# Eight experts after local attention: experts 2 to 7 in the order of their token counts, with slot lists cut by place

## The chip, the core and the metric

The kernel runs on one core of one Trainium2 chip. A core has five engines with queues of their own: TensorE (PE, with its weight loads shown apart as PEld), VectorE (DVE), ScalarE (ACT), GpSimd (POOL) and SyncE (SP), which here issues nearly all plain transfers. The metric is the time of one execution on the device in microseconds, as a median of runs; lower is better. Beside it stands one execution taken by the hardware profiler, from which all rows come.

## The reference

Attention over 4 batches, 8 heads and 768 positions, where a query sees the 96 positions up to its own and 8 global ones, with a bias by distance. Its output, 3072 tokens of 512 numbers, goes through a mixture of 8 experts, of which each token takes the two with the highest noisy logits:

```python
logits = x @ w_gate
noisy_logits = logits + np.log1p(np.exp(x @ w_noise)) * noise
top2 = np.argpartition(-noisy_logits, 2, axis=1)[:, :2]
# top2_w: softmax over the two chosen logits
for e in range(E):
    for k in range(2):
        mask = top2[:, k] == e
        h = np.maximum(x[mask] @ w1[e], 0.0)
        out[mask] += top2_w[mask, k, None] * (h @ w2[e])
```

w1[e] is 512 x 1024 and w2[e] 1024 x 512, in fp32. The experts share 6144 places in all, 768 each on average, but how many tokens an expert has is known only once the logits are.

## The kernel before

**Attention and routing.** Tokens go in 24 tiles of 128. While attention runs, route() works off five segments of tiles: it finds the two best experts of each token, counts per expert with matmuls against a triangle of ones (the running counts are kept in `carry`), and so gives each token a slot in its expert's list. A table of marks and entries multiplied on PE turns this round into `tab`, the token number of each slot; find() fills empty slots with rows of zeros and writes the result as integers, `ids`, of shape 128 x 8 experts x 8 tiles.

**An expert.** Every expert has 812 slots: a first list of 512 (4 tiles, `CA`) and a second of 300 (2 tiles and one of 44 rows, `CB`). gather() fetches the tokens of a tile by `ids` through POOL's queue; ready() and rest() split them into a high and a low fp16 half on DVE and ACT; turn() transposes a tile with a DMA that SP issues into `xx[0]` or `xx[1]`. The weights come as four quarters of 1 MB (`raw`, five buffers, load_w() on SP's queue), are scaled by powers of two (scales()) and split in halves too (split(): `w1h`, `w1l`, `w2h`, `w2l`). Products of halves replace fp32: three fp16 matmuls for one.

On PE an expert is: up(e, 0, f) for f = 0 to 7 (12 matmuls of 512 columns each, L857), up(e, 1, f) (12 of 300 columns), down(e, t) for 4 tiles (24 matmuls each, L890), then down_t(e, d) for d = 0 to 3, in which the weights stand still and the 300 slots move (24 matmuls each, L900), and back(e, t), which transposes its result again (4 transposes a tile, L911) while the next expert's up(e, 0, ...) runs. Behind each up step ACT writes `hh` = relu in fp16 (L867) and DVE `hl`, the rest (L868), out of one PSUM bank: bank "at" (two buffers) for even f, "sc" (three) for odd. put() (L874, L875) scales the rows and adds them to the output by an indirect DMA on POOL.

**What sets the order.** It is written out by hand: the loops over f, t and d at the end of the program say behind which PE step each step() of the next expert's weights, each gather, ready, rest and turn stands. An engine works its instructions off in that order. Expert 0 begins on tokens of the first 16 tiles, before all is routed, and experts 0 to 7 follow one another. At the end, if an expert had more tokens than slots, a serial part (behind the branch at L1032) computes those left over, by the counts in `carry` and the weights in `over`.

Of the kernel before, what the change touches and what calls it, by code (L numbers as in the profile page):

```python
# [20 lines left out]
P = 128  # L21
# [5 lines left out]
CAP = CA + CB  # L27
DUMP = 512
# [7 lines left out]
def tile_local_global_attention_then_moe(  # L36
# [60 lines left out]
    ids = consts.tile([P, E, TT + 1], I32, name="ids")  # L97
    ids0 = consts.tile([P, 1, TA], I32, name="ids0")
# [27 lines left out]
    asked = []  # L126

    def load_w(n=1):
        for _ in range(n):
# [3 lines left out]
            asked.append(order[len(asked)])  # L133
            if x == 1:
                t = wts.tile([P, KC, F // 2], F32, name="raw", tag="raw", bufs=5)
                src = w1[e, :, h * F // 2:(h + 1) * F // 2].rearrange("(k p) f -> p k f", p=P)
            else:
                t = wts.tile([P, FC // 2, Dm], F32, name="raw", tag="raw", bufs=5)
                src = w2[e, h * F // 2:(h + 1) * F // 2].rearrange("(k p) d -> p k d", p=P)
# [74 lines left out]
    def height(t):  # L214
        return P if t < TT - 1 else ML

    def rows(e, t):
        return (ids if e or t >= TA else ids0)[:height(t), e, t:t + 1]

    def gather(e, t, n=DUMP + N):  # L220
        xg[e, t] = gp.tile([height(t), Dm + E], F32, name="xg", bufs=5)
# [11 lines left out]
    def ready(e, t):  # L233
        x = xg[e, t]
        m = height(t)
# [9 lines left out]
    def rest(e, t):  # L245
        x = xg.pop((e, t))
        m = height(t)
# [8 lines left out]
    def turn(e, t):  # L256
        nc.sync.dma_start_transpose(out=place(t, P if t < TT - 1 else MP), in_=xp.pop((e, t)))

    def turn_pe(e, t, ps=None):
        x = xp.pop((e, t))  # L260
        m = height(t)
# [42 lines left out]
    def route(r):  # L304
# [80 lines left out]
        nc.vector.scalar_tensor_tensor(over[:, a:z], po, float(CAP), wd, op0=OP.is_ge, op1=OP.mult)  # L385
# [42 lines left out]
        if r + 1 == len(SEG):  # L428
            find(ids, slice(0, E), slice(0, TT + 1))
# [12 lines left out]
    with ExitStack() as actx:  # L442
# [114 lines left out]
        def route_consts():  # L557
# [21 lines left out]
            for x in tab, l1, wv:  # L579
                nc.vector.memset(x, 0.0)  # L580

# [259 lines left out]
    with ExitStack() as mctx:  # L841
# [9 lines left out]
        def up(e, c, f, spared=False, between={}):  # L851
            ps = (bank("sc", 3) if f % 2 else bank("at", 2))[:, :hh[c].shape[2]]
            fs = slice(f * P, (f + 1) * P)
            n = 0
            for k in range(KC):
                for w, x in ((w1h, 0), (w1h, KC), (w1l, 0)):
                    nc.tensor.matmul(ps, w[e % 2][:, k, fs], xx[c][:, x + k, :hh[c].shape[2]], start=n == 0, stop=n == 3 * KC - 1)  # L857
# [3 lines left out]
            if spared:  # L861
                h = mw.tile([P, 512], F32, name="h")[:, :hh[c].shape[2]]
                nc.scalar.activation(h, ps, AF.Relu)
                nc.scalar.activation(hh[c][:, f], h, AF.Copy)
                nc.gpsimd.tensor_sub(hl[c][:, f], h, hh[c][:, f])
                return
            nc.scalar.activation(hh[c][:, f], ps, AF.Relu)  # L867
            nc.vector.scalar_tensor_tensor(hl[c][:, f], ps, 0.0, hh[c][:, f],  # L868
                                           op0=OP.max, op1=OP.subtract)

        def put(e, t, ps):
            m = height(t)
# [21 lines left out]
        def down_t(e, d):  # L894
            ps = bank("av", 2)[:, :CB]
            cols = slice(d * P, (d + 1) * P)
            n = 0
            for f in range(FC):
                for w, x in ((w2h, hh), (w2h, hl), (w2l, hh)):
                    nc.tensor.matmul(ps, w[e % 2][:, f, cols], x[1][:, f], start=n == 0, stop=n == 3 * FC - 1)  # L900
                    n += 1
            if d % 2:
                nc.vector.tensor_copy(yt[:, d], ps)
            else:
                nc.scalar.activation(yt[:, d], ps, AF.Copy)

        def back(e, t):
            m = height(TA + t)
# [57 lines left out]
        for f in range(FC):  # L966
# [20 lines left out]
        for e in range(1, E):  # L987
            last = e + 1 == E
            for f in range(FC):
                up(e, 0, f)  # L990
                if f < TB:
# [5 lines left out]
            weigh(e, 0, TT)  # L997
            for f in range(FC):
# [5 lines left out]
                if not last:  # L1004
                    if f in (4, 6):
                        ready(e + 1, f // 2 - 2)
                    if f in (5, 7):
                        rest(e + 1, f // 2 - 2)
                        turn(e + 1, f // 2 - 2)
                        gather(e + 1, f // 2 + 3)  # L1010
            steps = [(down, t) for t in range(TA)]
            steps_t = [(down_t, d) for d in range(KC)]
            for j, (f, t) in enumerate(steps_t + steps if last else steps + steps_t):
                f(e, t)
                if not last:
                    if j < TA + TB - 2:
                        ready(e + 1, j + 2)
                    step(e + 1, [1, 3, 3, 3, 1, 1, 1, 1][j])
                    if j < TA + TB - 2:
                        rest(e + 1, j + 2)  # L1020
                        turn(e + 1, j + 2)
                elif j in (KC, KC + 1, KC + 2):
# [5 lines left out]
    nc.vector.tensor_scalar(cf[:, :E], carry[:1], -float(CAP), 0.0, op0=OP.add, op1=OP.max)  # L1028
# [3 lines left out]
    with tc.If(left > 0), tc.tile_pool(name="lc", bufs=1) as lc:  # L1032
        nc.sync.dma_start(past.rearrange("(t p) e -> p t e", p=P), over)
        for e in range(E):
            n = nc.values_load(more[0:1, e:e + 1], min_val=0, max_val=N)
            with tc.If(n > 0):
# [4 lines left out]
                with tc.For_i(0, NT, 1) as i:  # L1041
# [20 lines left out]
                    for f in range(FC):  # L1062
                        nc.tensor.matmul(ps, ht[:, f], wb[:, f], start=f == 0, stop=f == FC - 1)
                    nc.scalar.activation(y, ps, AF.Copy, scale=r[:, e:e + 1])
# [42 lines left out]
```

## Time and profile before

| | |
|---|---|
| median of 3 runs | 744.93 us (744.08 to 745.27) |
| the profiled execution | 747.32 us, its span 745.6 us |
| PE busy, of the span | 715.7 us (96%), 6199 matmuls |
| DVE busy | 485.2 us (65%) |
| ACT busy | 346.4 us (46%) |
| POOL busy | 208.3 us (28%) |
| mean granted clock of PE | 0.982 |

The span runs from the first to the last instruction. Busy times of single matmuls overlap, since matmuls are pipelined: what a group of them costs is read from the chain of waits, whose pieces don't overlap, and not from the mean of one. A DVE row whose bracket says "idle before" shows how long the engine waited ahead of it and for whom.

### The profile page before, as it was taken

How to read it: one execution, taken by the hardware profiler on the slowest of the kernel's cores; microseconds unless marked ns; L12 is line 12 of the kernel's file. 1: busy time of each engine (PE TensorE's matmuls, PEld its weight loads, DVE VectorE, ACT ScalarE, POOL GpSimd, SP SyncE). 2: the span in 40 equal slices, each digit the busy share in tenths (PEclk: the TensorE clock that was granted, in tenths of full speed). 3: DMA queues.
4: the chain of work that ended last, by engine and by line, in shares of the span. 5: the costliest groups of instructions: out<-in, count | busy, mean ns of one | idle time of the engine just before them, and what ended most of it. 6: DMA issues, size and time to landing. Idle time of an engine off the chain costs nothing.

```text
span 745.6 us, 16302 instructions
## 1 busy us (share of the span) xinstructions
PE 715.7 (96%) x6199; PEld 448.6 (60%) x6199; DVE 485.2 (65%) x1655; ACT 346.4 (46%) x744; POOL 208.3 (28%) x201
## 2 busy tenths in 40 slices
PE   7999978996999999999999999999999999999995
PEld 5887757775446746465555646464655556464762
DVE  7658896888697828655873767286558737672500
ACT  5887776675435434524252433345242524333401
POOL 2000184230346650313223121503132231212014
PEclk9999998898999999999999999999999999999999
DMA  7889794765519783784597558539945973642015
GB/s 223 267 271 279 241 291 146 231 224 207 207 41 166 218 179 114 136 156 93 163 144 127 170 104 183 106 116 132 161 94 161 137 134 119 99 69 34 1 20 75
DMA packets 107671, 112.56 MB, mean 151 GB/s; under 512 B 53216, under 2 KB 66224, under 8 KB 107584
## 3 DMA queue, kind: packets, MB, share of 16 engines
q1 hardware_dynamic: 95104, 84.25, 41.8%
q0 software_dynamic: 11936, 26.92, 21.0%
q8 instruction: 51, 0.84, 0.5%
q14 instruction: 36, 0.29, 0.1%
q10 hardware_dynamic: 544, 0.26, 0.1%
HBM read 71.61 MB, written 28.10 MB: 134 GB/s over the span
## 4 chain that ended last, share of the span: by engine, by line
PE 70%; issue 12%; DVE 11%; POOL 2%; ACT 2%; DMA 1%; POOLq 0%; SPq 0%; ACTq 0%; DVEq 0%
PE av L890 17%; PE at L857 15%; PE sc L857 14%; PE av L900 10%; PE av L664 4%; PE at L637 3%; POOL out_dram L875 2%; PE sc L616 2%; DVE ns L623 2%; DVE entry L409 1%; PE sc L285 1%; DVE wmx L149 1%; PE sc L293 1%; PE lg L299 1%; DVE xr L672 1%
## 5 line engine op out<-in xcount | busy, mean ns | idle before, releaser
L875 POOL DMA_INDIRECT out_dram<-y,ids x56 | 88.2, 1575 | 213.0 <-ACT y L874 208.8
L857 PEld LDWEIGHTS <-w1h 128*128 128x128 f16 x1024 | 99.8, 98 | 68.5 <-issue 0.8
L857 PE MATMUL at<-xx,w1h 128*128 128x300 f16 (+1 forms) x512 | 127.9, 338 | 0.0
L857 PE MATMUL sc<-xx,w1h 128*128 128x300 f16 (+1 forms) x512 | 126.2, 335 | 0.0
L222 POOL DMA_INDIRECT xg<-xd,ids x56 | 57.5, 1027 | 162.0 <-DVE hl L868 124.2
L890 PE MATMUL av<-w2h,hh 128*128 128x512 f16 x256 | 97.1, 379 | 0.0
L890 PE MATMUL av<-w2l,hh 128*128 128x512 f16 x256 | 97.0, 379 | 0.0
L890 PE MATMUL av<-w2h,hl 128*128 128x512 f16 x256 | 97.0, 379 | 0.0
L626 ACT ACTIVATE a<-ns,mx 128x168 f32<-128x168 f32 (+1 forms) x192 | 69.6, 421 | 41.3 <-DVE mx L623 40.5
L857 PE MATMUL at<-xx,w1l 128*128 128x512 f16 (+1 forms) x256 | 86.3, 337 | 0.0
L857 PE MATMUL sc<-xx,w1l 128*128 128x512 f16 (+1 forms) x256 | 85.8, 335 | 0.0
L890 PEld LDWEIGHTS <-hh 128*128 128x128 f16 x512 | 49.5, 98 | 56.0
L868 DVE SCALAR_TENSOR_TENSOR hl<-sc,hh 128x300 f16<-128x300 f32 (+1 forms) x63 | 36.3, 577 | 67.5 <-ACT hh L867 67.4
L149 DVE TENSOR_REDUCE wmx<-raw 128x1 f32<-128x1024 f32 x64 | 76.6, 1207 | 0.0
L900 PE MATMUL av<-hh,w2h 128*128 128x300 f16 x256 | 74.6, 291 | 0.0
L900 PE MATMUL av<-hh,w2l 128*128 128x300 f16 x256 | 74.3, 290 | 0.0
L900 PE MATMUL av<-hl,w2h 128*128 128x300 f16 x256 | 74.1, 290 | 0.0
L857 PEld LDWEIGHTS <-w1l 128*128 128x128 f16 x512 | 50.3, 98 | 37.9 <-issue 0.5
L867 ACT ACTIVATE hh<-at 128x300 f16<-128x300 f32 (+1 forms) x62 | 31.1, 502 | 89.1 <-PE at L857 89.1
L868 DVE SCALAR_TENSOR_TENSOR hl<-at,hh 128x300 f16<-128x300 f32 (+1 forms) x62 | 35.5, 573 | 52.6 <-ACT hh L867 52.6
L242 ACT ACTIVATE xp<-xg,up 128x512 f16<-128x512 f32 x48 | 34.5, 719 | 70.8 <-DVE up L240 60.6
L900 PEld LDWEIGHTS <-w2h 128*128 128x128 f16 x512 | 50.0, 98 | 16.5
(173 smaller groups left out, 1242.2 us busy)
## 6 DMA issues: line engine op xcount, KB each, us to landing
raw<-in_w SPq DMA_DIRECT2D x32, 1024.0 KB, 7.5
out_dram<-zero SPq DMA_DIRECT2D x14, 512.0 KB, 6.1
vs<-in_v SPq DMA_DIRECT2D x24, 260.0 KB, 3.4
xd<-xr SPq DMA_DIRECT2D x24, 256.0 KB, 7.9
qs<-in_q SPq DMA_DIRECT2D x23, 256.0 KB, 5.3
ks<-in_k SPq DMA_DIRECT2D x19, 272.0 KB, 9.5
vp<-in_v SPq DMA_DIRECT2D x20, 195.0 KB, 3.8
ks<-in_k SPq DMA_DIRECT2D x4, 464.0 KB, 4.6
```

The lines of the kernel that those rows point to most:

```text
L149: nc.vector.tensor_reduce(m[:, i:i + 1], t[:, i % 2 * n:(i % 2 + 1) * n], op=OP.max, axis=AX.X, apply_absolute_value=True)
L222: nc.gpsimd.indirect_dma_start(out=xg[e, t], out_offset=None, in_=xd[:n], in_offset=bass.IndirectOffsetOnAxis(ap=rows(e, t), axis=0), boun ...
L242: nc.scalar.activation(y[:m, :Dm], x[:, :Dm], AF.Copy, scale=u)
L626: nc.scalar.activation(A[m][:, s * w:(s + 1) * w], ns[:, s, :w], AF.Exp, bias=mx[:, s:s + 1], scale=-1.0)
L637: nc.tensor.transpose(ps[:, j * P:(j + 1) * P], x[:, a:a + P], ident)
L664: nc.tensor.matmul(ps[y * Q:(y + 1) * Q, h % 4], w, t, start=id(x) in first, stop=id(x) in final, tile_position=(r, y * Q))
L857: nc.tensor.matmul(ps, w[e % 2][:, k, fs], xx[c][:, x + k, :hh[c].shape[2]], start=n == 0, stop=n == 3 * KC - 1)
L867: nc.scalar.activation(hh[c][:, f], ps, AF.Relu)
L868: nc.vector.scalar_tensor_tensor(hl[c][:, f], ps, 0.0, hh[c][:, f], op0=OP.max, op1=OP.subtract)
L875: ins = nc.gpsimd.indirect_dma_start(out=out, out_offset=bass.IndirectOffsetOnAxis(ap=rows(e, t), axis=0), in_=y, in_offset=None, bounds_c ...
L890: nc.tensor.matmul(ps, x[0][:, f, cols], w[e % 2][:, f], start=n == 0, stop=n == 3 * FC - 1)
L900: nc.tensor.matmul(ps, w[e % 2][:, f, cols], x[1][:, f], start=n == 0, stop=n == 3 * FC - 1)
```

## The change

**Places.** The loop variable e now is a place and not an expert. Places 0 and 1 hold experts 0 and 1. Places 2 to 7 hold experts 2 to 7, the one with the most tokens first. A place has a fixed number of slots, `CAPS`: 812, 812, 812, 788, 776, 772, 768 and 768, so the second list has 300, 300, 300, 276, 264, 260, 256 and 256 slots; places 3 to 5 have a last tile of 20, 8 and 4 rows, places 6 and 7 have six tiles. The widths of up(e, 1, f), down_t() and of ACT's and DVE's work behind them follow.

**Ranking.** rank() computes on DVE, from `carry`, how many experts have more tokens than each, with ties broken by number, and makes `pick` (place x expert, one 1 in each row) and `turni` (the expert of each place, as an integer). permute() sorts the table of slots by place: for each place a product with `pick` and a sum. find() now writes `flat` in fp32 and the first two experts' `ids` are copied from it. limits() gives each expert's number of slots for the serial part at the end.

**Weights by register.** Before the first load of place 2, SP loads six registers from `turni`, and the weights of places 2 to 7 are addressed by them. The second of the two loads that stood in up(0, 1, 0) now stands in up(0, 1, 3).

**A token's weight** for places from 2 on is no longer a column of the gathered row but the sum of its product with `pick`.

```diff
+CAPS = (CAP, CAP, CAP, 788, 776, 772, 768, 768)
...
+            if e >= 2 and not regs:
+                regs.extend(nc.values_load(turni[0:1, j:j + 1], engines=(mybir.EngineType.SP,), min_val=0, max_val=E - 1)
+                            for j in range(2, E))
+            i = slice(e, e + 1) if e < 2 else ds(regs[e - 2], 1)
...
+    def rank():
+
+        nc.vector.tensor_scalar(cnt, carry, float(E), None, op0=OP.mult)
+        nc.vector.tensor_sub(cnt, cnt, iota_e[:, 0])
+        for e in range(2):
+            nc.vector.memset(cnt[:, e:e + 1], float((3 - e) * E * N))
+        sh = [P, E, E]
+        nc.vector.tensor_tensor(pick, cnt[:, None, :].to_broadcast(sh), cnt[:, :, None].to_broadcast(sh), op=OP.is_gt)
+        nc.vector.tensor_reduce(turnf, pick, op=OP.add, axis=AX.X)
+        nc.vector.tensor_tensor(pick, iota_e[:, 0, :, None].to_broadcast(sh), turnf[:, None, :].to_broadcast(sh),
+                                op=OP.is_equal)
+        m = small.tile(sh, F32, name="m88")
+        nc.vector.tensor_mul(m, pick, iota_e[:, 0, None, :].to_broadcast(sh))
+        nc.vector.tensor_reduce(turnf, m, op=OP.add, axis=AX.X)
+        nc.vector.tensor_copy(turni, turnf)
+
+    def permute(a, z):
+        for e in range(a, z):
+            m = small.tile([P, TT, E], F32, name="m78")
+            nc.vector.tensor_mul(m, flat[:, :, :TT].rearrange("p e t -> p t e"),
+                                 pick[:, e, None, :].to_broadcast([P, TT, E]))
+            nc.vector.tensor_reduce(flat2[:, e, :TT], m, op=OP.add, axis=AX.X)
+        nc.vector.tensor_copy(ids[:, a:z, :TT], flat2[:, a:z, :TT])
...
-        nc.vector.tensor_copy(wv[:m, e, t:t + 1], x[:, Dm + e:Dm + e + 1])
+        if e < 2:
+            nc.vector.tensor_copy(wv[:m, e, t:t + 1], x[:, Dm + e:Dm + e + 1])
+        else:
+            w = gp.tile([P, E], F32, name="wm", bufs=2)[:m]
+            nc.vector.tensor_mul(w, x[:, Dm:], pick[:m, e])
+            nc.vector.tensor_reduce(wv[:m, e, t:t + 1], w, op=OP.add, axis=AX.X)
...
-        nc.vector.scalar_tensor_tensor(over[:, a:z], po, float(CAP), wd, op0=OP.is_ge, op1=OP.mult)
+        nc.vector.tensor_copy(over[:, a:z], po)
...
-            find(ids, slice(0, E), slice(0, TT + 1))
+            find(flat, slice(0, E), slice(0, TT + 1))
+            nc.vector.tensor_copy(ids[:, :2], flat[:, :2])
...
-            if f == 0:
-                load_w(2)
+            if f in (0, 3):
+                load_w()
             if f not in (0, 2):
                 step(1)
+            if f == 1:
+                rank()
+            if f == 5:
+                permute(2, 4)
...
-            weigh(e, 0, TT)
+            weigh(e, 0, tiles(e))
+            if e == 1:
+                permute(4, E)
+                limits()
```

On DVE, in expert 0's second up steps before (xx, xp, hl and w1l are the tiles named above; "sc" and "at" the PSUM banks):

```order
L868 SCALAR_TENSOR_TENSOR hl_4119<-sc,hh_4117 128x300
L208 SCALAR_TENSOR_TENSOR w1l_108<-raw,wsc,w1h_106 128x4x128
L868 SCALAR_TENSOR_TENSOR hl_4119<-at,hh_4117 128x300
L249 SCALAR_TENSOR_TENSOR xp<-xg,up,xp 128x512
L250 COPY wv<-xg 128x1
```

And at the same place in the changed kernel, from the same hl on (its line is L925 now):

```order
L925 SCALAR_TENSOR_TENSOR hl_4135<-sc,hh_4133 128x300
L221 SCALAR_TENSOR_TENSOR w1l_116<-raw,wsc,w1h_114 128x4x128
L238 TENSOR_SCALAR cnt<-carry 128x8
L239 TENSOR_TENSOR cnt<-cnt,iota_e 128x8
L241 MEMSET cnt 128x1 x2
L243 TENSOR_TENSOR pick<-cnt 128x64
L244 TENSOR_REDUCE turnf<-pick 128x8
L245 TENSOR_TENSOR pick<-iota_e,turnf 128x64
L248 TENSOR_TENSOR m_4801<-pick,iota_e 128x64
L249 TENSOR_REDUCE turnf<-m_4801 128x8
L250 CAST turni<-turnf 128x8
L925 SCALAR_TENSOR_TENSOR hl_4135<-at,hh_4133 128x300
```

rank() stands between the split of the second up step and the hl of the third. Four up steps later permute(2, 4) stands ahead of the last two hl, here in the changed kernel:

```order
L925 SCALAR_TENSOR_TENSOR hl_4135<-sc,hh_4133 128x300
L255 TENSOR_TENSOR m_4949<-flat,pick 128x56
L257 TENSOR_REDUCE flat_86<-m_4949 128x7
L255 TENSOR_TENSOR m_4952<-flat,pick 128x56
L257 TENSOR_REDUCE flat_86<-m_4952 128x7
L258 CAST ids<-flat_86 128x2x7
L925 SCALAR_TENSOR_TENSOR hl_4135<-at,hh_4133 128x300
L925 SCALAR_TENSOR_TENSOR hl_4135<-sc,hh_4133 128x300
```

Before, these three hl followed one another. On SP's queue in the same stretch, before (raw is a quarter of an expert's weights; the transposes are tiles 0 and 1, then 2, then 3 of expert 1):

```order
L257 DMA_TRANSPOSE xx_109<-xp 128x8x128 x2
L140 DMA raw<-in_w 128x4x512 x2
L257 DMA_TRANSPOSE xx_109<-xp 128x8x128
L140 DMA raw<-in_w 128x4x512
L257 DMA_TRANSPOSE xx_109<-xp 128x8x128
```

And in the changed kernel, from the transpose of tile 2 to that of tile 3 (the ISA rows are the registers' limits and address arithmetic; the load and its two rows stand there six times, of which the first and the last are shown):

```order
L310 DMA_TRANSPOSE xx_117<-xp 128x8x128
L144 TENSOR_LOAD turni
L144 ISA x2
...
L144 TENSOR_LOAD turni
L144 ISA x2
L153 ISA
L153 DMA raw<-in_w 128x4x512
L153 ISA
L153 DMA raw<-in_w 128x4x512
L310 DMA_TRANSPOSE xx_117<-xp 128x8x128
```

Two weight loads instead of one now stand directly ahead of the transpose of tile 3, behind six register loads that wait for `turni`.

## Rows read from the trace of the kernel before

**Rows 1.** The chain of waits in order of time, one expert: start us, us, what.
```profile
395.65 2.59 PE at L857 x12
...
404.30 0.44 PE sc L911 x4
...
418.21 1.53 PE at L857 x12
...
451.69 12.27 PE av L900 x96
```
**Rows 2.** One expert's stretch: busy us of each engine, clock, DMA share, GB/s.
```profile
395.65:463.96 68.31, 68.31 (x404) 39.44 (x402) 43.31 (x92) 27.13 (x48) 18.19 (x14) 1.00 0.66 140
```
**Rows 3.** The chain of waits in order of time, expert 0.
```profile
228.49 0.45 PE lg L264 x8
...
246.76 12.27 PE av L900 x96
259.03 1.08 PE at L857 x5
```
**Rows 4.** DVE in order of time, small instructions: start us, us, what.
```profile
194.84 1.32 DVE L328 SCALAR_TENSOR_TENSOR p<-p,t 128x32 f32<-128x32 f32 x6
...
216.69 0.22 DVE L438 TENSOR_TENSOR find<-find,tab 128x64 f32<-128x64 f32 x1
216.94 0.22 DVE L439 TENSOR_TENSOR ids<-find,find 128x64 int32<-128x64 f32 x1
```
**Rows 5.** DVE in order of time, expert 0's second up steps.
```profile
240.55 0.75 DVE L208 SCALAR_TENSOR_TENSOR w1l<-raw,wsc,w1h 128x512 f16<-128x512 f32 x1
241.22 0.46 DVE L868 SCALAR_TENSOR_TENSOR hl<-at,hh 128x300 f16<-128x300 f32 x1
...
244.52 0.47 DVE L868 SCALAR_TENSOR_TENSOR hl<-sc,hh 128x300 f16<-128x300 f32 x1 [1.15 <-ACT hh L867]
...
247.33 0.45 DVE L868 SCALAR_TENSOR_TENSOR hl<-sc,hh 128x300 f16<-128x300 f32 x1
...
248.20 0.47 DVE L868 SCALAR_TENSOR_TENSOR hl<-sc,hh 128x300 f16<-128x300 f32 x1
```
**Rows 6.** PE in order of time, the first transposed down of expert 0.
```profile
248.65 0.29 PE L900 MATMUL av<-hl,w2h 128*128 128x300 f16 x1
...
249.42 0.29 PE L900 MATMUL av<-hl,w2h 128*128 128x300 f16 x1
```
**Rows 7.** POOL in order of time, first and last of eight.
```profile
246.12 1.57 POOL L205 TENSOR_SCALAR raw<-raw,wsc 128x512 f32<-128x512 f32 x1 [6.08 <-ACT w1h L203]
...
256.99 1.16 POOL L206 TENSOR_TENSOR w1l<-raw,w1h 128x512 f16<-128x512 f32 x1
```
**Rows 8.** One DVE line: ns min/median/max, first and last start us, shapes.
```profile
L385 DVE SCALAR_TENSOR_TENSOR over<-po,wd x5: 184/196/1090, 85.4 to 207.3; 128x40 f32<-128x40 f32 x2, 128x32 f32<-128x32 f32 x2, 128x48 f32<-128x48 f32 x1
```
**Rows 9.** SP's queue in order of time: start us, us, what.
```profile
239.51 1.25 SPq L140 DMA_DIRECT2D raw<-in_w  x2
242.40 4.64 SPq L257 DMA_TRANSPOSE xx<-xp  x1
...
247.77 3.13 SPq L257 DMA_TRANSPOSE xx<-xp  x1
```
**Rows 10.** A register load at the program's end: ns min/median/max, first and last start.
```profile
L1031 SPq TENSOR_LOAD <-more x1: 473/473/473, 716.9 to 716.9; - x1
...
L1031 SPq FUSED_REGOPS  x1: 188/188/188, 717.5 to 717.5; - x1
```
**Rows 11.** DMA issues: out<-in queue op xcount, KB each, median us to landing.
```profile
raw<-in_w SPq DMA_DIRECT2D x32, 1024.0 KB, 7.5
...
xx<-xp SPq DMA_TRANSPOSE x42, 4.6
```
**Rows 12.** DVE in order of time, expert 1's third up step of the second list.
```profile
287.94 0.47 DVE L868 SCALAR_TENSOR_TENSOR hl<-at,hh 128x300 f16<-128x300 f32 x1
```
**Rows 13.** The chain of waits in order of time, expert 1.
```profile
290.77 1.53 PE at L857 x12
```

More of the change, by code (lines that the diff above doesn't have):

```diff
@@ L97, in tile_local_global_attention_then_moe @@
     ids = consts.tile([P, E, TT + 1], I32, name="ids")
+    flat = consts.tile([P, E, TT + 1], F32, name="flat")
+    flat2 = consts.tile([P, E, TT + 1], F32, name="flat2")
+    pick = consts.tile([P, E, E], F32, name="pick")
+    cnt = consts.tile([P, E], F32, name="cnt")
+    room = consts.tile([P, E], F32, name="room")
+    capv = consts.tile([P, E], F32, name="capv")
+    turnf = consts.tile([P, E], F32, name="turnf")
+    turni = consts.tile([P, E], I32, name="turni")
     ids0 = consts.tile([P, 1, TA], I32, name="ids0")
@@ L212, in tile_local_global_attention_then_moe, with tiles, height, padded @@
     xg, xp = {}, {}
-    def height(t):
-        return P if t < TT - 1 else ML
+    def tiles(e):
+        return -(-CAPS[e] // P)
+    def height(e, t):
+        return min(P, CAPS[e] - t * P)
+    def padded(e, t):
+        return -(-height(e, t) // 16) * 16
+    def rank():
[19 more added lines that the diff above has]
+        nc.vector.tensor_copy(ids[:, a:z, :TT], flat2[:, a:z, :TT])
+    def limits():
+        m = small.tile([P, E, E], F32, name="m88")
+        nc.vector.tensor_mul(m, pick, room[:, :, None].to_broadcast([P, E, E]))
+        nc.vector.tensor_reduce(capv, m.rearrange("p a b -> p b a"), op=OP.add, axis=AX.X)
     def rows(e, t):
-        return (ids if e or t >= TA else ids0)[:height(t), e, t:t + 1]
+        return (ids if e or t >= TA else ids0)[:height(e, t), e, t:t + 1]
     def gather(e, t, n=DUMP + N):
-        xg[e, t] = gp.tile([height(t), Dm + E], F32, name="xg", bufs=5)
+        xg[e, t] = gp.tile([height(e, t), Dm + E], F32, name="xg", bufs=5)
         nc.gpsimd.indirect_dma_start(
@@ L256, in turn @@
     def turn(e, t):
-        nc.sync.dma_start_transpose(out=place(t, P if t < TT - 1 else MP), in_=xp.pop((e, t)))
+        nc.sync.dma_start_transpose(out=place(t, padded(e, t)), in_=xp.pop((e, t))[:padded(e, t)])
     def turn_pe(e, t, ps=None):
         x = xp.pop((e, t))
-        m = height(t)
+        m = height(e, t)
         ps = (spare_bank(bank16) if ps is None else ps)[:, :2 * KC * m].rearrange("p (k t) -> p k t", k=2 * KC)
@@ L580, in route_consts @@
                 nc.vector.memset(x, 0.0)
+            for e in range(E):
+                nc.gpsimd.memset(room[:, e:e + 1], float(CAPS[e]))
         def empty_rows():
@@ L851, in up @@
         def up(e, c, f, spared=False, between={}):
-            ps = (bank("sc", 3) if f % 2 else bank("at", 2))[:, :hh[c].shape[2]]
+            z = CAPS[e] - CA if c else CA
+            ps = (bank("sc", 3) if f % 2 else bank("at", 2))[:, :z]
             fs = slice(f * P, (f + 1) * P)
@@ L856, in up @@
                 for w, x in ((w1h, 0), (w1h, KC), (w1l, 0)):
-                    nc.tensor.matmul(ps, w[e % 2][:, k, fs], xx[c][:, x + k, :hh[c].shape[2]], start=n == 0, stop=n == 3 * KC - 1)
+                    nc.tensor.matmul(ps, w[e % 2][:, k, fs], xx[c][:, x + k, :z], start=n == 0, stop=n == 3 * KC - 1)
                     n += 1
@@ L894, in down_t @@
         def down_t(e, d):
-            ps = bank("av", 2)[:, :CB]
+            z = CAPS[e] - CA
+            ps = bank("av", 2)[:, :z]
             cols = slice(d * P, (d + 1) * P)
@@ L990, in tile_local_global_attention_then_moe @@
                 up(e, 0, f)
-                if f < TB:
+                if f < tiles(e - 1) - TA:
                     back(e - 1, f)
```

45 lines of the change are left out of this document (25 added, 20 removed).

## The prediction

> **What bounds the kernel now.** I read the page's busy table first, then the chain of waits in order of time for the second half of the run, then the stretches by stage, and last the engines' own timelines around the place of the edit. In the chain, from about 220 us to the last matmul, nearly every piece is TensorE (PE), piece upon piece without a gap. One expert is a fixed pattern: eight "up" steps of 2.59 us over 512 slots, eight of 1.53 us over 300 slots, four "down" tiles, and 12.27 us for the transposed "down" over 300 slots [rows 1]. The stretch of one expert lasts 68.31 us with PE busy for all of it, VectorE (DVE) for 43.3 us and GpSimd (POOL) for 18.2 us [rows 2]. So columns taken from PE come off the end one for one, as long as no other engine becomes late; and work put on DVE costs only where DVE is already just in time.
>
> **What it removes.** An "up" step of 12 matmuls takes 2.59 us at 512 columns and 1.53 us at 300 [rows 1]: 215.8 and 127.5 ns a matmul, or 88.3 ns for 212 columns, 0.417 ns a column. An expert has 8 x 12 matmuls "up" and 96 "down" over its second list of slots, 192 in all. The places' lists go from 300 to 300, 276, 264, 260, 256 and 256 columns (places 2 to 7): 24 + 36 + 40 + 44 + 44 = 188 columns, times 192 is 36,096 columns, times 0.417 ns is 15.04 us. Places 6 and 7 also lose their seventh tile and its four transposes, 0.44 us each time [rows 1], 0.88 us. The seventh tile of places 3 to 5 stays at its 0.44 us, since its 128 moving columns stay. Together PE loses 15.92 us.
>
> That the price per column holds down to 256 is not seen in this stage. Eight fp16 transposes of 128 columns, each with weights of its own, take 0.45 us [rows 3], 56 ns each; so loading weights does not hold a matmul at 109 ns, which is what 256 columns come to. The bounds are 0 (the pace stays at 127.5 ns) and 15.04; I take 15.04, as the row is well below.
>
> The Trainium skill speaks against this part: "TensorE: Matmul & The Clock Gate", section Back-to-back issue gap, gives a real stream of weight loads and matmuls 81 ns at 128 columns and 131 ns at 512. That is 0.13 ns a column, by which the 36,096 columns would be worth an estimated 4.7 us. Rows 1 differ at both widths, and the measurement decides.
>
> **What it adds on DVE while expert 0 ends.** rank() is ten instructions behind the second "up" step of expert 0's second list, and permute(2, 4) five behind the sixth. Six chained small instructions took 1.32 us, 0.22 each; two on 64 columns started 0.25 apart [rows 4]. Ten of them are 8 x 0.23 plus two short memsets of 0.1: 2.0 us. Five are 1.1 us.
>
> Are they covered? Behind rank() DVE's next idle time is the 1.15 us at 244.52 [rows 5], but it waits there for ScalarE, which had waited for DVE's "ready" of the next expert's tile; that chain moves with DVE, so the idle time covers nothing. The last hl (the low halves that "down" reads) ends at 248.20 + 0.47 = 248.67 [rows 5], and the matmul that reads it starts at 249.42 [rows 6]: 0.75 us of cover. All above that PE waits out, in the first transposed "down" of expert 0.
>
> POOL adds to it. From 246.12 to 258.15 it runs eight instructions without a pause [rows 7], which start behind ScalarE and so move along with the rest; permute(2, 4) falls into them. A DVE instruction with two SBUF inputs that usually takes 0.20 us took 1.09 once [rows 8], 0.9 more. With two such multiplies in permute that is 0 to 1.8 us; I take 1.0, the middle. The lag is 2.0 + 1.1 + 1.0 = 4.1, and the wait 4.1 - 0.75 = 3.35 us. Its bounds: 15 instructions at 0.11 (half the row's pace) and nothing held, 1.65 - 0.75 = 0.9; at 0.25 and both held, 5.55 - 0.75 = 4.8.
>
> The Trainium skill has the lock behind this ("SBUF — State Buffer", section SBUF: two separate sides): a DVE instruction with two SBUF inputs and a GpSimd one that reads SBUF exclude each other for the whole instruction. By that rule each multiply could be held for a whole POOL instruction, up to 2.0 us here, and the estimate of the wait would end at 1.65 + 4.0 + 1.45 - 0.75 = 6.35 us; rows 8 show no hold that long.
>
> **What it adds on SP.** Six register loads stand in SP's queue behind the transpose of expert 1's tile 2, and wait there for rank(). Before, that transpose started at 242.40 and held SP for 4.64, and tile 3's started at 247.77 for 3.13 [rows 9]. Now tile 2 starts some 2.0 later, 244.4 to 249.0; six loads at 0.473 + 0.188 [rows 10] are 4.0, to 253.0; two weight loads at 1.25 / 2 each [rows 9] to 254.3; then tile 3. Its first reader is expert 1's first "up", at 259.03 [rows 3] plus the 3.35 of waiting: 262.4. A transpose lands 4.6 after its issue in the median, a weight load 7.5 [rows 11]. Alone, tile 3 lands at 258.9; behind the second weight load, issued at 253.7 and landing at 261.2, perhaps at 262 to 265. I charge 0.3, between 0 and 3.0. The moved weight load itself (expert 2's first quarter) is first read by DVE after 280 and has time.
>
> **What else it adds.** After expert 1's first list come eleven more DVE instructions, 2.4 us. The hl of its third "up" step ends at 287.94 + 0.47 and its PSUM bank is wanted again at 290.77 [rows 12, 13], 2.36 us later: the cover just suffices, and the price is 0 to 0.4, taken as 0. For 40 tiles a copy of 0.15 becomes two instructions, some 0.3 more each, 2 us an expert against 25 us of idle DVE [rows 2]: nothing. POOL's eight memsets stand in the attention stage, where nothing waits for them, and the copy in place of the product for "over" is one small DVE instruction for another.
>
> **The sum.** 15.92 - 3.35 - 0.3 = 12.3 us. The profiled execution took 747.32 us, 1.7 of it outside its span of 745.6, and would take 735.0. The median of the runs without a profile, 744.93, is 2.4 lower, and gives 732.6 us.
>
> **Rivals.**
> 1. *All is hidden.* DVE's lag is absorbed, and only the columns count: 744.93 - 15.92 = 729.0. For it: 25 us of idle DVE per expert [rows 2]. Against: the 0.75 us at this place [rows 5, 6].
> 2. *SP becomes the bound once.* Tile 3 lands behind two weight loads of 1 MB and PE waits again at expert 1's first "up", by 3 us: 735.6; with 4 us more of queue, 739.6. For it: the two weight loads now directly ahead of the transpose. Against: the queue is emptier in the 4 us before.
> 3. *Narrower matmuls do not run faster* (the other side): below 300 columns another pace holds, say that of the weight loads, and PE saves 0.88 but waits 3.65: 747.7, slower. It decides once less than 18% of the 15.04 us comes, a 256-column matmul above 124 ns instead of 109. For it: no row of this stage is narrower than 300. Against: the 56 ns of rows 3.
> 4. *Loads addressed by register are slow.* An expert's four weight loads and seven transposes (some 3.1 each, 22) share one queue; in the shorter period of 64.4 us each load may hold it for 10.6. Every microsecond more costs 4 per expert, 24 in all: at 12 us the time is 744.93 - 12.3 + 33 = 766. Against: they land in 7.5 with other traffic [rows 11], and a register adds only an address.
> 5. *The places are too small* and the slow path behind the experts runs. Counted from the reference on its inputs, experts 2 to 7 have 751, 806, 768, 763, 761 and 772 tokens; in falling order they leave 6, 16, 8, 9, 7 and 17 slots free. Each expert beyond its place would cost 24 tiles of serial work, far over 50 us.
>
> **How the numbers follow.** Forecast 0.67, rival 1 0.14, rival 2 0.12, rivals 3 and 4 0.03 each, rival 5 0.01. About 0.2% (1.5 us) is what a measurement tells from no change. Faster: the first three, 0.93, and a part of 3 and 4 where they fall short, 0.94; same 0.01; slower 0.05. The forecast's own bounds are 744.93 - 15.0 = 729.9 and 744.93 - 8.1 = 736.8 (4.8 and 3.0 together). With rival 1 below, the range is 728.7 to 736.8.
>
> **What would show it.** An "up" step of 256 columns at 1.31 us and the last transposed "down" at 10.5 us show the columns; 1.53 us there makes rival 3. A gap of 2 to 4 us on PE in the first transposed "down" of expert 0, released by DVE's hl, shows the lag; none shows rival 1. A gap at expert 1's first "up", released by a DMA, shows rival 2. The stretches of places 6 and 7 should be 3.96 us shorter. I am wrong if PE has gaps in the later experts, or if the runs lie outside 728.7 to 736.8.

## The result and the profile after

The changed kernel takes 736.82 us (median of 4 runs, 734.1 to 739.81) against 745.1 us for the kernel before beside it (4 runs, 744.08 to 748.38): a ratio of 0.9871 with the interval 0.9837 to 0.9905. By the two medians that is 8.3 us less, by the ratio 9.6 (7.1 to 12.1). On the 744.93 us from which the forecast started the ratio gives 735.3 us; the forecast was 732.6 within 728.7 to 736.8, so the time lies near the upper end of the range. The direction came out as predicted, and so did the gain from the columns and the wait in expert 0; the gain as a whole is smaller by a fifth (ratio) to a third (medians) than the 12.3 us of the forecast. Later runs of both kernels (the first experiment) gave 9.9 us by their medians.

The profiled execution of the changed kernel took 739.81 us, its span 738.1 against 745.6. PE is busy for 703.6 us (95%) instead of 715.7, DVE for 491.7 instead of 485.2.

Stretches from one expert's first up matmul to that of the next, places 1 to 6. The columns are those of [rows 2]:
```profile
265.15:334.83 69.68, 68.86 (x404) 39.39 (x402) 47.22 (x112) 27.29 (x48) 18.58 (x14) 1.00 0.68 144
334.83:403.14 68.31, 68.31 (x404) 39.48 (x402) 44.60 (x99) 27.15 (x48) 18.38 (x14) 1.00 0.65 129
403.14:469.88 66.74, 66.53 (x404) 39.42 (x402) 44.19 (x99) 27.11 (x48) 18.36 (x14) 1.00 0.67 141
469.88:536.08 66.20, 65.56 (x404) 39.40 (x402) 44.00 (x99) 27.07 (x48) 18.29 (x14) 1.00 0.64 135
536.08:601.16 65.08, 65.08 (x404) 39.36 (x402) 42.22 (x93) 26.35 (x47) 17.00 (x13) 1.00 0.65 142
601.16:665.92 64.76, 64.76 (x404) 39.38 (x402) 42.16 (x93) 26.32 (x47) 16.96 (x13) 1.00 0.50 94
```
Before, each was 68.31 us. The second number of a line is PE's busy time: where it is below the length, PE waited. Set against the price of the removed columns (192 matmuls x columns x 0.417 ns; the four seventh-tile transposes of place 6 fall into the stretch of place 7, so that stretch loses 0.88):

| stretch | before | after | difference | priced columns and transposes | rest |
|---|---|---|---|---|---|
| place 1 | 68.31 | 69.68 | +1.37 | 0 | +1.37 |
| place 2 | 68.31 | 68.31 | 0 | 0 | 0 |
| place 3 | 68.31 | 66.74 | -1.57 | -1.92 | +0.35 |
| place 4 | 68.31 | 66.20 | -2.11 | -2.88 | +0.77 |
| place 5 | 68.31 | 65.08 | -3.23 | -3.20 | -0.03 |
| place 6 | 68.31 | 64.76 | -3.55 | -3.52 | -0.03 |
| place 7, to the end | 76.87 | 72.18 | -4.69 | -4.40 | -0.29 |

So the columns came at the full price where nothing waits, and 2.49 us were given back in places 1, 3 and 4. The rest lies in expert 0, whose stretch grew from 73.63 to 78.85 us, by 5.2; 4.4 of it are told next, the other 0.8 lies ahead of the change, where routing still runs (from the first up matmul to the first of the second list it is 49.87 us, before 49.12).

What PE waited for from 190 us on, without the 1.1 us for routing's `entry` that stand in both profiles (engine, line, releaser: us, times, longest):
```profile
PE av L958 <- DVE hl L925: 2.5, 2, 1.7
PE av L958 <- DVE yt L961: 1.0, 3, 0.6
PE sc L173 <- DVE d L170: 0.5, 1, 0.5
PE at L914 <- DVE hl L925: 0.2, 1, 0.2
```
The same question to the kernel before names `entry` alone and none of these four. The first is the forecast's wait. PE in order of time there, which answers [rows 6]:
```profile
250.39 0.29 PE L958 MATMUL av<-hh,w2h 128*128 128x300 f16 x1
251.51 0.29 PE L958 MATMUL av<-hl,w2h 128*128 128x300 f16 x1 [0.83 <-DVE hl L925]
251.64 0.29 PE L958 MATMUL av<-hh,w2l 128*128 128x300 f16 x1
251.77 0.29 PE L958 MATMUL av<-hh,w2h 128*128 128x300 f16 x1
253.72 0.41 PE L958 MATMUL av<-hl,w2h 128*128 128x300 f16 x1 [1.66 <-DVE hl L925]
253.92 0.46 PE L958 MATMUL av<-hh,w2l 128*128 128x300 f16 x1
254.17 0.46 PE L958 MATMUL av<-hh,w2h 128*128 128x300 f16 x1
...
257.10 0.29 PE L958 MATMUL av<-hh,w2h 128*128 128x300 f16 x1
```
Two things are to be seen. From start to start the second wait took 253.72 - 251.77 = 1.95 us where a matmul takes 0.13, so it cost 1.82 and not the 1.66 in the bracket (the bracket counts from the modelled end of the matmul ahead); the first cost 1.00 the same way, together 2.82. And behind it matmuls start 0.25 apart instead of 0.13: PE ran at 1.2 GHz, the lower of its two levels. The stretches say so (columns as in [rows 2]):
```profile
250.50:253.70 3.20, 0.72 (x5) 0.29 (x3) 3.06 (x10) 1.95 (x5) 3.12 (x3) 0.98 0.34 60
253.70:257.10 3.40, 3.38 (x15) 2.04 (x15) 3.33 (x8) 1.03 (x2) 3.23 (x4) 0.51 1.03 383
```
The clock is the third number from the end: PE was busy for 0.72 of 3.20 us, and then had a granted clock of 0.51 for 3.4 us. Fourteen matmuls took 3.38 us from 253.72 to 257.10 instead of 14 x 0.128 = 1.79: 1.6 us more, which the forecast didn't have.

DVE in order of time, which answers [rows 5]: rank() from 243.00, permute(2, 4) from 251.38 (L255 to L258), and the two hl (L925) that PE waits for:
```profile
243.00 0.17 DVE L238 TENSOR_SCALAR cnt<-carry 128x8 f32<-128x8 f32 x1
...
244.82 0.17 DVE L250 CAST turni<-turnf 128x8 int32<-128x8 f32 x1
244.90 0.46 DVE L925 SCALAR_TENSOR_TENSOR hl<-at,hh 128x300 f16<-128x300 f32 x1
...
248.19 0.47 DVE L925 SCALAR_TENSOR_TENSOR hl<-sc,hh 128x300 f16<-128x300 f32 x1 [1.14 <-ACT hh L924]
...
251.01 0.45 DVE L925 SCALAR_TENSOR_TENSOR hl<-sc,hh 128x300 f16<-128x300 f32 x1
251.38 0.23 DVE L255 TENSOR_TENSOR m<-flat,pick 128x56 f32<-128x56 f32 x1
251.65 0.21 DVE L257 TENSOR_REDUCE flat<-m 128x7 f32<-128x56 f32 x1
251.90 0.78 DVE L255 TENSOR_TENSOR m<-flat,pick 128x56 f32<-128x56 f32 x1
252.71 0.21 DVE L257 TENSOR_REDUCE flat<-m 128x7 f32<-128x56 f32 x1
252.96 0.34 DVE L258 CAST ids<-flat 128x14 int32<-128x14 f32 x1
253.21 0.46 DVE L925 SCALAR_TENSOR_TENSOR hl<-at,hh 128x300 f16<-128x300 f32 x1
```
rank() holds DVE from 243.00 to 244.90, 1.90 us, permute(2, 4) from 251.38 to 253.21, 1.83. The idle time of 1.14 us ahead of the hl at 248.19 stayed, as in [rows 5]: it covers nothing. The first wait (0.83) ends with the hl at 251.01, which stands ahead of permute and is late by rank() alone; the second ends with the hl at 253.21, late by permute.

SP (first the register loads: ns min/median/max, first and last start; then its queue in order of time), which answers [rows 9, 10]:
```profile
L144 SPq TENSOR_LOAD <-turni x6: 262/270/1067, 247.4 to 251.1; - x6
L144 SPq FUSED_REGOPS  x6: 147/147/186, 248.5 to 251.4; - x6
```
```profile
246.08 1.25 SPq L310 DMA_TRANSPOSE xx<-xp  x1
251.83 1.06 SPq L153 DMA_DIRECT2D raw<-in_w  x2
252.99 2.84 SPq L310 DMA_TRANSPOSE xx<-xp  x1
```
The six loads lie between 247.4 and 251.6, 4.2 us, and tile 3's transpose starts at 252.99. Its data landed at 260.92 by the trace's record of its semaphore, 7.9 us after the start of its issue, and expert 1's first up, which reads them, starts at 265.15 without a wait. The weight loads, now addressed by register, land after 7.4 us in the median, before after 7.5 [rows 11].

### The profile page after: what moved, and what is told of

Same layout as the page of the kernel before. It is cut to its first block, busy times and chain, and to the rows that moved or that the text cites. A ratio compares the mean times of both kernels' runs of the same rounds, so it can differ in the third digit from the quotient of the medians.

```text
span 738.1 us, 16394 instructions
## 1 busy us (share of the span) xinstructions
PE 703.6 (95%) x6191; PEld 449.0 (61%) x6191; DVE 491.7 (67%) x1714; ACT 343.3 (47%) x740; POOL 203.2 (28%) x205
## 5 line engine op out<-in xcount | busy, mean ns | idle before, releaser
L914 PE MATMUL at<-xx,w1h 128*128 128x512 f16 (+5 forms) x512 | 124.7, 334 | 0.2 <-DVE hl L925 0.2
L914 PE MATMUL sc<-xx,w1h 128*128 128x512 f16 (+5 forms) x512 | 122.8, 330 | 0.0
L914 PE MATMUL at<-xx,w1l 128*128 128x512 f16 (+5 forms) x256 | 85.3, 333 | 0.0
L914 PE MATMUL sc<-xx,w1l 128*128 128x512 f16 (+5 forms) x256 | 84.5, 330 | 0.0
L925 DVE SCALAR_TENSOR_TENSOR hl<-sc,hh 128x512 f16<-128x512 f32 (+5 forms) x63 | 35.5, 564 | 66.4 <-ACT hh L924 66.4
L958 PE MATMUL av<-hl,w2h 128*128 128x300 f16 (+4 forms) x256 | 72.5, 283 | 2.5 <-DVE hl L925 2.5
L958 PE MATMUL av<-hh,w2h 128*128 128x300 f16 (+4 forms) x256 | 72.6, 284 | 1.0 <-DVE yt L961 1.0
L958 PE MATMUL av<-hh,w2l 128*128 128x300 f16 (+4 forms) x256 | 72.4, 283 | 0.0
L925 DVE SCALAR_TENSOR_TENSOR hl<-at,hh 128x512 f16<-128x512 f32 (+5 forms) x62 | 34.8, 560 | 51.7 <-ACT hh L924 51.7
L720 PE MATMUL av<-vs,at 128*64 128x65 f32 (+1 forms) x768 | 60.0, 233 | 0.0
```

Source lines behind the costliest of these rows:

```text
L720: nc.tensor.matmul(ps[y * Q:(y + 1) * Q, h % 4], w, t, start=id(x) in first, stop=id(x) in final, tile_position=(r, y * Q))
L914: nc.tensor.matmul(ps, w[e % 2][:, k, fs], xx[c][:, x + k, :z], start=n == 0, stop=n == 3 * KC - 1)
L925: nc.vector.scalar_tensor_tensor(hl[c][:, f, :z], ps, 0.0, hh[c][:, f, :z], op0=OP.max, op1=OP.subtract)
L958: nc.tensor.matmul(ps, w[e % 2][:, f, cols], x[1][:, f, :z], start=n == 0, stop=n == 3 * FC - 1)
```

## The experiments

The theory after the first look had three parts: the removed columns are worth their full 15.9 us; DVE instructions put ahead of an hl, a d or a yt that is only just in time are waited for in full; and the stretch of half clock behind the wait is a part of the price. The rivals: part of the columns' price is lost elsewhere (register-addressed loads, SP), or the waits are absorbed. Letters in an expectation are those which it defines itself. All runs of one group share their runs of the kernel before: 749.32 us for the first four, 748.49 for the others.

**The changed kernel again**, without an edit, as the base of the others.

> The changed kernel once more, for a tighter time beside its variants. Every theory: about 736.8 us, 8 below the kernel before; its runs so far spread over 5.7 us, those of before over 4.3. If the spread comes from the stretches of half clock in the attention stage, which lie elsewhere in each execution (the changed kernel's profile is 1.7 us late there already), other runs of it spread alike and their median may move by 1 or 2.

739.41 us (736.45 to 743.03), ratio 0.9866 (0.9836 to 0.9897): 9.9 us less. Its profile has the same waits, 0.83 and 1.66 us, but no half clock behind them. Columns as in [rows 2]:
```profile
250.50:253.70 3.20, 2.13 (x16) 1.36 (x14) 3.13 (x8) 3.20 (x7) 2.41 (x2) 1.00 0.76 141
253.70:257.10 3.40, 1.98 (x16) 1.52 (x16) 3.26 (x9) 0.75 (x2) 3.32 (x4) 1.00 0.72 223
```
So the half clock is not a fixed part of the price: it comes in some executions.

**The order written in.** The rank of the experts on these inputs stands as a constant; rank(), permute(), limits() and the registers are left out, and a token's weight is one copy again.
```diff
+PL = (0, 1, 3, 7, 4, 5, 6, 2)
...
-            i = slice(e, e + 1) if e < 2 else ds(regs[e - 2], 1)
+            i = slice(PL[e], PL[e] + 1)
...
-            nc.vector.tensor_mul(w, x[:, Dm:], pick[:m, e])
-            nc.vector.tensor_reduce(wv[:m, e, t:t + 1], w, op=OP.add, axis=AX.X)
+        nc.vector.tensor_copy(wv[:m, e, t:t + 1], x[:, Dm + PL[e]:Dm + PL[e] + 1])
...
-            if f == 1:
-                rank()
-            if f == 5:
-                permute(2, 4)
```

> The same shorter lists, but the order of the experts (0, 1, 3, 7, 4, 5, 6, 2) is written into the program, which holds for these inputs alone: no ranking, no sorting of the table, no registers, and a token's weight is one copy again. Theory A (the columns are worth their full 15.04 us, the transposes 0.88, and what is missing is lost to the ranking's instructions on VectorE): 744.9 - 15.9 = 729.0, between 728.5 and 730.0, with no wait of TensorE in expert 0's transposed down. Theory B (shorter lists make waits of their own, on hl and yt, since VectorE has less time per step): 731 to 733.

733.28 us (731.21 to 733.88), ratio 0.9776 (0.9754 to 0.9798): by the medians 16.0 us less than before, where columns and transposes were priced at 15.9; theory B of the expectation (12 to 14 less) is out. Places 1, 4 and 6 in its profile:
```profile
261.09:329.40 68.31, 68.31 (x404) 39.40 (x402) 43.56 (x94) 27.12 (x48) 18.39 (x14) 1.00 0.74 155
464.07:529.58 65.51, 65.51 (x404) 39.38 (x402) 42.79 (x92) 26.96 (x48) 18.09 (x14) 1.00 0.68 135
594.66:659.43 64.77, 64.77 (x405) 39.37 (x403) 41.10 (x87) 26.18 (x47) 16.96 (x13) 1.00 0.50 102
```
PE fills every stretch, and place 4's 65.51 is 2.80 under 68.31 for 36 columns priced at 2.88. The columns are worth their price. What the changed kernel lacks of it is the price of the ranking, in which the pairs of instructions for a token's weight are counted.

**The ranking alone**, with all eight places at the old size.
```diff
-CAPS = (CAP, CAP, CAP, 788, 776, 772, 768, 768)
+CAPS = (CAP,) * 8
```

> Ranking, sorting and weights by register as in the changed kernel, but all eight lists keep their 812 slots. Theory A: the cost side alone. 2.5 us of waits on hl, 1.4 us of half clock behind them, and about 0.7 to 1.9 of small waits later: 744.9 + 4.6 to 5.8 = 749.5 to 750.7. Without the clock's part it would be 748.1 to 749.3. Theory B (the ranking costs no more than the 2.5, the rest is due to the shorter lists): 747.4.

755.16 us (753.42 to 756.23), ratio 1.0075 (1.0055 to 1.0095): 5.8 us slower than before (4.1 to 7.1). Its profile has the waits for hl (2.5 us in two, and 0.2) and for d (0.5), hardly one for yt (0.15), and its stretches of places 2 to 6 are 68.31. The 2.5 of theory B are out. Gain and price add up: 16.0 - 5.8 = 10.2 against the 9.9 of both together, to within a microsecond or two; a cost of 1.1 us that only both together have (places 3 and 4, told below) is too small to be seen in this sum. No half clock stands behind its waits either. By its trace the price is 2.82 us in expert 0 and 1.36 in place 1 (69.67 - 68.31); that the runs show 1.6 more than this is within their interval.

**The ranking moved into expert 1.** rank() stands behind its first first-list up step, the permutations behind steps 1, 2 and 4; weights of places from 2 on are asked for once they are ranked.
```diff
-            if f == 1:
-                rank()
-            if f == 5:
-                permute(2, 4)
...
+                if e == 1 and f == 0:
+                    rank()
+                    n, held[0] = held[0], None
+                    load_w(n)
+                if e == 1 and f in (1, 2, 4):
+                    a = {1: 2, 2: 4, 4: 6}[f]
+                    permute(a, a + 2)
+                    if f == 4:
+                        limits()
```

> As the changed kernel, but rank() stands behind the first up step of expert 1's first list, and the sorting behind its second, third and fifth, where VectorE is idle for 2.3 us between two hl; the three weight loads of place 2 that were asked for earlier are held back until then. Theory A: no wait in expert 0's transposed down, so the clock stays at its upper level there, and no wait on hl in expert 1: 736.8 - 2.5 - 1.4 - 0.7 = 732.2, between 731 and 733. Rival (the registers or the later weight loads are what costs): 735 to 737, with a wait on raw weights or on a DMA in expert 1 or 2.

734.27 us (733.2 to 736.82), ratio 0.981 (0.9786 to 0.9833): 15.1 us less than the kernel before, 5.1 less than the changed one, where 4.6 were expected. It does the same work as the changed kernel and beats both. DVE there, and what PE still waits for that the kernel before doesn't:
```profile
264.26 0.69 DVE L928 SCALAR_TENSOR_TENSOR hl<-at,hh 128x512 f16<-128x512 f32 x1 [1.36 <-ACT hh L927]
264.87 0.16 DVE L241 TENSOR_SCALAR cnt<-carry 128x8 f32<-128x8 f32 x1
...
266.68 0.17 DVE L253 CAST turni<-turnf 128x8 int32<-128x8 f32 x1
267.27 0.69 DVE L928 SCALAR_TENSOR_TENSOR hl<-sc,hh 128x512 f16<-128x512 f32 x1 [0.42 <-ACT hh L927]
```
```profile
PE av L961 <- DVE yt L964: 0.8, 2, 0.6
```
Behind rank() DVE still idles for 0.42 us until ACT has the next hh: here the ten instructions lie in time that DVE has left, in expert 0's second list they didn't. Place 1 is back at 68.31 us. The six register loads stand in this kernel too. By the medians it is 1.0 us above the order written in, and its waits for yt are 0.8 of that, so these runs leave no price for the loads that they could show.

**rank() twice**, a double dose in the place of the change.
```diff
             if f == 1:
                 rank()
+                rank()
```

> The changed kernel with rank() written twice in a row at its place (ten DVE instructions more, 1.90 us by the profile of the changed kernel; the same result twice). Theory A (each microsecond that DVE lags beyond its cover in expert 0's second list is waited for once, in the first transposed down of expert 0): the two waits there go from 2.49 to 4.4 us, the time is 1.9 us above the changed kernel, about 8.0 under the kernel before, ratio 0.989. Theory B (a wait costs more than its length, since a stretch of half clock follows it, as in the first profile of the changed kernel, where 3.4 us behind it ran at 0.51): 3.3 us or more above the changed kernel, ratio 0.991 or more, and the granted clock behind the wait falls under 1. Rival C (DVE catches up before the end): no more than 0.3 above.

742.58 us (740.49 to 742.95), ratio 0.9914 (0.9894 to 0.9935): 5.9 us under the kernel before, by the two ratios 3.6 us above the changed kernel, though the intervals of the two ratios leave anything from 0 to 7. The trace is plainer: the two waits in the transposed down stayed at 0.83 and 1.66, and a new one stands earlier, in the seventh up step, which wants the PSUM bank that the late hl of the third frees:
```profile
247.69 0.41 PE L914 MATMUL at<-xx,w1h 128*128 128x300 f16 x2 [1.80 <-DVE hl L925]
```
From the first matmul of the second list to this one it is 11.14 us (236.55 to 247.69), in the changed kernel 9.24 (236.17 to 245.41): PE lost 1.90 us more there for 1.90 more of DVE, so once the cover is spent, one for one. The place at which the lag is paid had been expected wrongly, the amount not. In this profile half clock follows the waits, which makes the rest of the 3.6 (clock in the third number from the end, as in [rows 2]):
```profile
255.50:259.00 3.50, 3.00 (x13) 1.80 (x13) 3.43 (x9) 1.03 (x2) 3.42 (x3) 0.52 0.93 341
```

**permute(2, 4) later**, behind expert 1's second first-list up step; rank() stays.
```diff
-            if f == 5:
-                permute(2, 4)
...
+                if e == 1 and f == 1:
+                    permute(2, 4)
```

> The changed kernel with permute(2, 4) moved from behind expert 0's sixth second-list up step to behind expert 1's second first-list up step; rank() stays. Theory A: the second of the two waits, 1.66 us, goes and the first, 0.83, which comes ahead of permute, stays: time 1.7 us under the changed kernel, ratio about 0.984. Theory B (half clock follows a wait of 2.5 us): 1.7 and up to 1.4 more, 3.1 under it, ratio 0.9825. Rival C (rank() alone makes the whole wait and permute fits beside it): the wait stays at 2.4 and the time where it was, 0.9866.

738.48 us (737.32 to 741.4), ratio 0.9865 (0.9842 to 0.9888): by time nothing that can be told from the changed kernel's 0.9866, so the expected 1.7 was not seen there. In the trace the second wait is gone and the first is left, as expected, and a new one stands at expert 1's first up:
```profile
255.89 0.29 PE L958 MATMUL av<-hl,w2h 128*128 128x300 f16 x1 [0.84 <-DVE hl L925]
...
266.69 0.59 PE L914 MATMUL at<-xx,w1h 128*128 128x512 f16 x2 [0.30 <-issue]
```
From start to start it costs 0.46 us. This row names no releaser, but PE's sequencer does: ahead of the same up it waits for a semaphore, here for 2.69 us from 263.9, in the changed kernel for 0.05 (ns, then first and last start; first here, then the changed kernel):
```profile
L914 PEldq EVENT_SEMAPHORE  x1: 2692/2692/2692, 263.9 to 263.9; - x1
L914 PEldq EVENT_SEMAPHORE  x1: 51/51/51, 262.9 to 262.9; - x1
```
In the trace that semaphore is raised by tile 3's transpose, issued at 257.30: its last update comes at 266.60, 9.3 us later, and the wait ends at 266.64. So this pause is at the place and by the transfer of the second rival, at 0.46 us instead of 3. The same transfer took 7.5 us in the kernel before, with one weight load directly ahead of it, and 7.8 to 8.2 in the four profiles with both waits on hl, with two ahead of it; there PE came later, in the changed kernel 12.2 us after the issue (252.99 to 265.15) instead of 9.4. Why it took 9.3 here is not shown.

**The weights of tokens later**, on top of the ranking in expert 1: the two small instructions for `wv` of tiles 4 to 6 stand together behind the second transposed down.
```diff
-        else:
+        elif t < 4:
             w = gp.tile([P, E], F32, name="wm", bufs=2)[:m]
...
+        else:
+            late.append((e, t, x))
...
+                    if j == 5:
+                        weights_late()
```

> The version that ranks during expert 1 (734.27 us, ratio 0.981), with the product and sum for wv of tiles 4 to 6 of experts 2 to 7 issued together behind the second transposed down instead of inside each rest(). Theory A (the 0.16 us instructions that rest() gained lie directly ahead of the yt copy that PE waits for): the two waits for yt, 0.21 and 0.63 us, go from the trace and the time is 0.8 us lower, 733.4, ratio 0.980; by time alone this is at the edge of what can be told. Rival (yt is late because of the 1.2 us reduction of raw ahead of it, whatever the small ones do): both waits stay within 0.1.

734.81 us (731.22 to 736.39), ratio 0.9808 (0.9783 to 0.9833): by time the same as the ranking in expert 1. In the trace both waits for yt are gone, and the stretches of places 3 and 4 are 66.36 and 65.41 us instead of 66.73 and 66.18. DVE ahead of the yt copy, first in the ranking in expert 1, then here:
```profile
526.21 0.73 DVE L300 SCALAR_TENSOR_TENSOR xpb<-xg,up,xpb 4x512 f16<-4x512 f32 x1
526.87 0.15 DVE L305 TENSOR_TENSOR wm<-xg,pick 4x8 f32<-4x8 f32 x1
527.05 0.15 DVE L306 TENSOR_REDUCE wv<-wm 4x1 f32<-4x8 f32 x1
527.13 0.41 DVE L964 COPY yt<-av 128x264 f32<-128x264 f32 x1
```
```profile
527.34 0.73 DVE L310 SCALAR_TENSOR_TENSOR xpb<-xg,up,xpb 4x512 f16<-4x512 f32 x1
528.00 0.41 DVE L976 COPY yt<-av 128x264 f32<-128x264 f32 x1
```
The pair of 0.15 us instructions ahead of yt, and the pairs like it shortly before, had been enough to make PE wait; the rival of the expectation (the reduction ahead of them) is out, since the reduction stayed and the waits went.

**The kernel before, once more**, for its trace.

> The kernel before, once more with a profile. In its first profile expert 0's first list began at 189.03 us; in the five profiles of kernels with the change, in whole or in part, 1.7 to 3.6 us later, although the attention stage is the same but for eight memsets on POOL. Theory A (the stretches of half clock fall elsewhere in each execution): here too it begins 1.7 to 3.6 us later than in the first profile, with stretches of half clock in other places. Rival (the change itself delays the attention stage by 2 us): it begins within 0.5 of 189.03.

751.42 us in its profiled execution. The first weight load of expert 0's first up starts at 190.1 us, where it was 185.0 in the first profile of this kernel:
```profile
L857 PEld LDWEIGHTS <-w1h x1024: 95/98/293, 190.1 to 707.3; 128*128 128x128 f16 x171
```
Without any edit the attention stage took 5 us longer, more than in any of the five profiles that had raised the question (their first up matmul lies at 186.3 to 189.6, here at 190.27). The 189.03 us of the expectation is not where that list began: in the first profile its first up matmul starts at 185.24, and the five are 1.1 to 4.4 us later. The rival isn't needed: the kernel before alone spreads over 5 us, and a delay by the change that is smaller than this can't be seen in single profiles. Spans of single profiles may therefore be compared from expert 0 on only. In the second profile of each kernel the changed one gains 749.7 - 738.0 = 11.7 us, of which 190.27 - 189.07 = 1.2 lie ahead of expert 0: 10.5 are the change.

## Why the prediction was nearly right

The time lay in the range, near its upper end, and the wait in expert 0 came where it was forecast. But one of the prediction's own signs of being wrong appeared as well: PE has gaps in later experts, in places 1, 3 and 4.

**Columns and transposes: 15.92, measured 16.0** (the order written in, by medians; by the interval of its ratio 15.1 to 18.4). The pace holds down to 256 columns: in the stretch of place 6, 44 columns gave 3.55 us where 3.52 were priced, and an up step there takes 1.31 us (623.72 to 625.03), as the prediction had said. The rival of narrower matmuls is out. The Trainium skill's issue gap ("TensorE: Matmul & The Clock Gate", section Back-to-back issue gap), by which the columns would be worth an estimated 4.7 us, does not hold for this stream: 3.55 us over 192 x 44 columns are 0.42 ns a column, not 0.13.

**The wait in expert 0: 3.35, measured 2.82.** rank() took 1.90 (2.0 were charged), permute 1.83 (2.1), and the cover was 0.9 instead of 0.75: the last hl that PE waited for is that of the seventh step and not of the eighth, and in the kernel before it ended at 248.16 and its reader started at 249.03. The wait on POOL was over-charged: the first multiply took 0.23, only the second 0.78, 0.55 more instead of 1.0 (the middle of the bounds 0 to 1.8 would have been 0.9). It ran beside POOL's L219, which began at 251.45 and took 1.15 us, and ended 0.08 after it (0.07 in the second profile). "SBUF — State Buffer", section SBUF: two separate sides, of the Trainium skill has a DVE instruction with two SBUF inputs and a GpSimd one that reads SBUF shut each other out: the one that starts first keeps the port until its end. The end of the second multiply agrees with that. Another row doesn't: the xp at 249.85 (L297, 1.17 us, two SBUF inputs too) began 0.05 after POOL's L218 (249.80, 1.57 us) and ended 0.35 before it; spans on POOL are rough. So that the lock is what lengthened the multiply is argued, not shown.

**SP: 0.3, measured 0.** The queue was about as long as worked out (4.2 us of register loads instead of 4.0), but the transposes held the queue for less (1.25 and 2.84 instead of 4.64 and 3.13), and PE came later. Tile 3 landed 7.9 us after its issue, at 260.92, with 4.2 us to spare. Before it had taken 7.5, so the median of 4.6 did not describe this transfer, and the second weight load ahead of it added less than a microsecond. With the wait shortened (permute(2, 4) later) a pause of 0.46 us appeared at just this place.

**"What else it adds: nothing": this is the step that failed.** It was to cost 0, at most 0.4; it cost 2.49 us. Place 1 lost 1.37 at three short pauses (hl, d and yt, listed with 0.2, 0.5 and 0.15 us). The first is the one that the prediction had looked at, and its cost from start to start, 0.3 us, is within the 0 to 0.4; d and yt had not been looked at. With permute(4, E) and limits() moved into DVE's idle time this went to 0, though the pairs in rest() stayed. Places 3 and 4 lost 1.12 to the pairs: against 25 us of idle DVE an expert they had been priced at nothing. Idle time was there, but not ahead of yt. At the end of rest() for a seventh tile DVE is just in time for the transposed down, and with fewer columns PE is there sooner: at 300 columns (place 2, and the ranking alone) the pairs cost nothing, without the pairs the narrow columns cost at most 0.1 (the order written in), and both together cost 0.35 and 0.77. Stretches that prepare a place of six tiles (places 5 and 6) show no such wait. The error was to take a mean over an expert as cover for a place that has none, which the same text had refused to do in expert 0. That the total still came near is in part luck: the 0.5 charged too much for the wait and the 0.3 for SP made up for 0.8 of the 2.49 that had no price.

**What had no term: half clock behind the wait**, 1.6 us in the first profile of the changed kernel. It is there in two of the four profiles with both waits (the first of the changed kernel and rank() twice) and not in the other two.

The sum with measured terms is 15.9 - 2.8 - 2.5 = 10.6 us without the half clock and 9.0 with it; the two measurements are 8.3 and 9.9 by medians, their intervals by the ratios 7.1 to 12.1 and 7.7 to 12.3. What stays open is why half clock follows the same waits in one execution and not in another.

## What to carry to other kernels

Cover for an added instruction is the idle time ahead of the one result that is waited for, not the engine's share of idle time; look for it at each place where the added instruction stands, the small ones in a helper above all. Work that is ready early and needed late should go where its engine waits for another anyway: the ten instructions of rank() cost nothing behind expert 1's first step, but 1.0 of their 1.9 us in the middle of expert 0, and ten more there, with the cover spent, all of theirs. Compare profiles of two kernels stage by stage from the first stage that the change touches, since stages ahead of it can differ by several microseconds in one and the same kernel.

## What the runs showed of the hardware

- A pause of PE can be followed by 3.4 us at half clock (0.51 and 0.52 in two profiles), which cost 1.6 us behind a wait of 2.8; in two other profiles the same pause was followed by full clock.
- The attention stage of the unchanged kernel ended 5 us later in one execution than in another. Part of that are places where short bursts of matmuls start 0.75 us apart, with PE idle for 0.2 to 0.45 us in between and no releaser named ("issue"): 1.5 us from 100 us on, of which the other profile has none there; the cause isn't known.
- Register loads on SP took 0.27 us in the median, the first one 1.07, with 0.15 of register work each: less than the 0.473 and 0.188 of the load at the program's end before. That load itself took 0.284 and 0.155 in the changed kernel's profile.
- The transpose of expert 1's tile 3 landed 7.5 us after its issue behind one weight load of 1 MB (the kernel before), 7.8 to 8.2 behind two in four profiles and 9.3 in a fifth; the median of all transposes of the kernel before was 4.6 [rows 11].
